# Cross-covariance attention and a mixture of adapters on one core: v in transfers of two pieces, four v buffers, paired stores, a new order

## The chip, the core and the metric

The kernel runs on one core of one Trainium2 chip. Five engines work side by side: TensorE (PE, with its weight loads shown as PEld), VectorE (DVE), ScalarE (ACT), GpSimd (POOL) and SyncE (SP). Transfers between main memory (HBM) and on-chip memory (SBUF) run on 16 DMA engines which all queues share. The metric is the device time of one execution in microseconds, as the median of several executions. The data type of inputs and output is float32.

## The reference

Four batches (B = 4), each with N = 6400 rows of C = 256 columns. The first half is attention across columns, not rows:

```
qn = q / (norm(q, axis=1) + 1e-6);  kn = k / (norm(k, axis=1) + 1e-6)
s = kn.T @ qn / tau                   # 256 x 256 per batch, sum over 6400 rows
a = softmax(s, axis=-1)
x = v @ a                             # 6400 x 256 per batch
```

The second half is a mixture of 8 low-rank adapters on the 25600 rows of x:

```
logits = x @ w_gate                   # 8 per row; the two largest are kept
w = softmax of the two
out = x + sum over the two of  w * (x @ A[e]) @ B[e]     # rank 16
```

So q, k and v are each read once (26.2 MB each) and the output is written once (26.2 MB).

## The kernel before, in words

**Tiling.** A batch's 6400 rows lie as 128 partitions x 50 chunks ("columns" in what follows: one column is 128 rows of 256 values). q and k of a batch come in three transfers each, of 17, 17 and 16 columns (`QK`, line 244; some are cut smaller by `PARTS`, line 460). v of a batch is worked on in five pieces of 10 columns; each piece comes in a transfer of its own (`V`, line 245). All these loads are issued by GpSimd at line 658 and change float32 to bfloat16 on the way, so half as many bytes are written as are read. Stores are issued by SyncE at line 1002, one for each piece of 10 columns, except that the last two pieces go out as 4, 4 and 2 columns (`FINE`, line 461).

**Steps.** For each column, `G` (lines 667 to 685) multiplies q and k into the 256 x 256 sum and, where the group of columns is not listed in `OFF` (line 463), also makes the squares of k and q on TensorE (lines 677 and 682). For groups in `OFF` the squares are made by ScalarE (`sq`, line 695) and added up by VectorE (`add`, line 701). When a batch's 50 columns are done, a chain of small steps makes the softmax (`n2`, `rsqrt`, `rq_ps`, `s`, `exp`, `aT`, `waA`, `a`). Then each v piece is transposed (`T`, line 859), copied out (`Te`), its gate logits are made (`log`, line 897), the gate steps run on VectorE and ScalarE, `Z` (line 950) makes x @ A, `Ze` scales it, `gzT` (line 973) transposes it, and five `Y` steps (lines 986 and 991) make the output of two columns each, which `Ye` copies into a y buffer. For the pieces in `MERGED` (line 470) `log` and `Z` are one step, `ZL` (line 883).

**Buffers.** Three v buffers of one piece each lie side by side in one tile (`VS`), and seven y buffers of one piece each in another (`Y`). There are six q/k buffers. A load is issued only when its buffer is free: a v buffer when the last `T` of its piece is done, a q/k buffer when the last `G` and square of its columns are done. A y buffer is free when its store has landed.

**Order.** The program is written out by a planner (`Plan`, line 69) that runs before the kernel is built: it places each step on an engine in an order that follows from its own estimates, the order of the loads (`WORDS`, line 449) and the list of buffers. On the chip each engine then works through its list strictly in that order. `HOLD` (line 456) makes a store wait until a named load has landed, although its data is ready; so reads go first and writes are kept for times in which there are few reads. `warm` steps (line 849) are matmuls without use, put where the planner expects TensorE to be idle, so that its clock is not lowered; `Clock` (line 33) decides where. GpSimd's queue has at most 8 loads under way (`OUT`).

Of the kernel before, what the change touches and what calls it, by code (L numbers as in the profile page):

```python
# [32 lines left out]
class Clock:  # L33


    WINDOW, FIRST, LOW, HIGH = 3.413, 0.31, 0.55, 0.8

    def __init__(self):
        self.busy, self.cold = [0.0], [True]

    def at(self, t):
        w = max(0, int((t - self.FIRST) / self.WINDOW) + 1)
# [6 lines left out]
    def took(self, t, us):  # L49

        end, w = t, self.at(t)
        while us > 1e-9:
            pace = 2.0 if self.cold[w] else 1.0
            step = min(us * pace, max(self.FIRST + w * self.WINDOW - end, 1e-6))
            self.busy[w] += step
            us -= step / pace
            end += step
            w = self.at(end)
        return end - t

    def idle(self, t):

        w = self.at(t)
        return t - self.FIRST - (w - 1) * self.WINDOW - self.busy[w] > self.SPARE

    SPARE = 0.8


class Plan:
# [171 lines left out]
PC = 10  # L241
NP = 5
UNITS = ((0, 4), (4, 4), (8, 2))
QK = ((0, 17), (17, 17), (34, 16))
V = (((0, 1), (1, 1), (2, 1), (3, 1), (4, 1)),) * 4
PAIRS = set()

GROUPS = ((0, 6), (6, 6), (12, 5), (17, 6), (23, 6), (29, 5), (34, 6), (40, 5), (45, 5))
ZUNITS = ((0, 3), (3, 3), (6, 2), (8, 2))
STORE = {"zl": 1, "bank": 6, "qk": 6, "v": 3, "vT": 4, "y": 7, "gate": 3, "gz": 4, "gzT": 4, "sq": 1, "ssq": 2, "port": 1}  # L250


def group_of(c):
# [187 lines left out]
def make_order(words):  # L441

    order = [("qk", 0, i) for i in range(len(QK))]
    for w in words.split():
# [1 line left out]
    return order  # L446


WORDS = ('q10 v00 v01 v02 q11 q12 v03 v04 v10 q20 v11 v12 q21 v13 q22 v14 q30 q31 v20 v21 v22 q32 v23 v24 v30 '
         'v31 v32 v33 v34')  # L450
HEAD = 5.05
COL = 1.024 * 1.17647 / 32
WARM = 150
AHEAD = 2.8

HOLD = {(0, 0): ('k', 2, 0), (0, 1): ('v', 3, 4), (0, 3): ('v', 2, 3), (1, 0): ('v', 3, 1), (1, 1): ('v', 3,
        1), (1, 3): ('v', 2, 3), (1, 4): ('v', 3, 0), (2, 2): ('v', 3, 2), (2, 3): ('v', 0, 4), (3, 0):
        ('k', 3, 2), (3, 1): ('k', 1, 1), (3, 2): ('v', 0, 1), (3, 4): ('k', 2, 1)}

PARTS = {(0, 0): ((0, 4), (4, 13)), (0, 2): ((34, 8), (42, 8)), (3, 2): ((34, 8), (42, 8))}  # L460
FINE = 2
SPLIT, SHARES = set(), ()
OFF = {(0, 0, 'k'), (0, 1, 'q'), (0, 2, 'q'), (0, 3, 'q'), (0, 5, 'q'), (0, 6, 'k'), (0, 8, 'k'), (1, 0,
        'k'), (1, 1, 'k'), (1, 2, 'k'), (1, 2, 'q'), (1, 3, 'q'), (1, 4, 'k'), (1, 5, 'q'), (1, 6, 'k'), (1,
        6, 'q'), (2, 0, 'k'), (2, 0, 'q'), (2, 3, 'q'), (2, 5, 'k'), (2, 5, 'q'), (2, 6, 'k'), (2, 7, 'q'),
        (2, 8, 'q'), (3, 0, 'k'), (3, 0, 'q'), (3, 1, 'q'), (3, 2, 'k'), (3, 2, 'q'), (3, 4, 'q'), (3, 5,
        'k'), (3, 6, 'k'), (3, 6, 'q'), (3, 7, 'k'), (3, 8, 'k')}
SQ = 0
SAFE = 0
MERGED = {(0, 1), (0, 4), (1, 0), (2, 1), (2, 2), (3, 0), (3, 2), (3, 3)}  # L470


def first_ahead(nc, names):
# [62 lines left out]
def kernel(  # L536
# [58 lines left out]
    def make_consts():  # L595
        ident = const.tile([P, P], BF16, name="ident")
        make_identity(nc, ident)
        W["ident"] = ident
        W["ident32"] = const.tile([P, P], FP32, name="ident32")
        nc.vector.tensor_copy(W["ident32"], ident)  # L600
        ones = const.tile([P, P], FP32, name="ones")
        nc.vector.memset(ones, 1.0)
        W["ones"] = ones
        neg = const.tile([P, 1], FP32, name="neg_inv_tau")
        nc.vector.memset(neg, -inv_tau)
        W["neg"] = neg
        W["zeros"] = const.tile([P, 256], BF16, name="zeros")
        nc.vector.memset(W["zeros"], 0.0)
        nc.scalar.activation(scrap[:, 0:1], neg[0:1, :], ACT.Exp)

    scrap = const.tile([1, 16], BF16, name="scrap")
# [128 lines left out]
    def do_rsqrt(s, b):  # L740
        n2 = st[b]["n2"]
        for x, w in enumerate("kq"):
            part = held.get(("bank", ("n2p", w, b)))
            if part is None:
                continue
            if all((b, g, w) in OFF for g in range(len(GROUPS))):
                nc.vector.tensor_copy(n2[:, x, :], part)
            else:
                nc.vector.tensor_tensor(out=n2[:, x, :], in0=part, in1=n2[:, x, :], op=OP.add)

        r = bat.tile([P, 2, CC], FP32, name="r0")
        nc.vector.tensor_scalar(out=r.bitcast(I32), in0=n2.bitcast(I32), scalar1=-0.5,
                                scalar2=float(0x5F1FFFF9), op0=OP.mult, op1=OP.add)
        for it, (c1, c0) in enumerate(((-0.703952253, 1.681914351), (-0.5, 1.5))):
            sq = bat.tile([P, 2, CC], FP32, name=f"sq{it}")
            nc.vector.tensor_tensor(out=sq, in0=r, in1=r, op=OP.mult)
            nc.vector.scalar_tensor_tensor(out=sq, in0=sq, scalar=c1, in1=n2,
                                           op0=OP.mult, op1=OP.mult)
            nxt = bat.tile([P, 2, CC], FP32, name=f"r{it + 1}")
            nc.vector.scalar_tensor_tensor(out=nxt, in0=sq, scalar=c0, in1=r,  # L760
                                           op0=OP.add, op1=OP.mult)
            r = nxt
        rqI = one.tile([P, CC, P], FP32, name="rqI")
        for ic in range(CC):
            nc.vector.tensor_scalar(out=rqI[:, ic, :], in0=W["ident"],
                                    scalar1=r[:, 1, ic:ic + 1], scalar2=None, op0=OP.mult)
        if inv_tau != 1.0:
            rt = bat.tile([P, CC], FP32, name="rt")
            nc.vector.tensor_scalar(out=rt, in0=r[:, 0, :], scalar1=inv_tau, scalar2=None, op0=OP.mult)
            st[b]["rk"] = rt  # L770
        else:
            st[b]["rk"] = r[:, 0, :]
        st[b]["rqI"] = rqI
# [72 lines left out]
        nc.scalar.copy(held["qk", (what, 0, 0), ""][:, 0:PARTS[0, 0][0][1], :], W[what])  # L846

    def do_warm(s, n):
        nc.tensor.matmul(bank(s, ("warm", n), [P, 512], FP32), W["ident"], W["zeros"][:, None, :].to_broadcast([P, 2, 256]),  # L849
                         start=True, stop=True)  # L850


# [16 lines left out]


    def gate_tiles(s, b, i):
        for part in ("log", "eq1", "lm", "t", "th", "mask", "g2"):
            sb(s, "gate", (b, i), [P, PC, E], FP32, part)
        for part in ("m1", "m2", "msum"):
            sb(s, "gate", (b, i), [P, PC], FP32, part)
# [30 lines left out]
    def gate_step(name):  # L906
        def f(s, b, i):
            if (b, i) in MERGED and name == "m1":
                gate_tiles(s, b, i)
            g = {part: held["gate", (b, i), part]  # L910
                 for part in ("log", "m1", "eq1", "lm", "m2", "msum", "t", "th", "mask", "g2")}
            if (b, i) in MERGED:
                g["log"] = held["zl", (b, i), ""][:, :, 0:E]
            wide = [P, PC, E]
            if name == "m1":
                nc.vector.tensor_reduce(out=g["m1"], in_=g["log"], axis=AX.X, op=OP.max)
            elif name == "eq1":
                nc.vector.tensor_tensor(out=g["eq1"], in0=g["log"], in1=g["m1"].to_broadcast(wide),
                                        op=OP.is_equal)
            elif name == "lm":  # L920
                nc.vector.scalar_tensor_tensor(out=g["lm"], in0=g["eq1"], scalar=-1e30, in1=g["log"],
                                               op0=OP.mult, op1=OP.add)
            elif name == "m2":
                nc.vector.tensor_reduce(out=g["m2"], in_=g["lm"], axis=AX.X, op=OP.max)
            elif name == "mask":
                nc.vector.tensor_tensor(out=g["mask"], in0=g["log"], in1=g["m2"].to_broadcast(wide),
                                        op=OP.is_ge)
            elif name == "msum":
                nc.vector.tensor_tensor(out=g["msum"], in0=g["m1"], in1=g["m2"], op=OP.add)
            elif name == "t":  # L930

                nc.vector.scalar_tensor_tensor(out=g["t"], in0=g["log"], scalar=2.0,
                                               in1=g["msum"].to_broadcast(wide),
                                               op0=OP.mult, op1=OP.subtract)
            elif name == "th":
                nc.scalar.activation(g["th"], g["t"], ACT.Tanh, scale=0.5)
            else:

                nc.vector.scalar_tensor_tensor(out=g["g2"], in0=g["th"], scalar=1.0, in1=g["mask"],
                                               op0=OP.add, op1=OP.mult)  # L940
# [14 lines left out]
    def do_Ze(s, b, i, u):  # L955
# [4 lines left out]
        for h in range(n // 2):  # L960
            nc.vector.tensor_tensor(  # L961
                out=pairs[:, h].rearrange("p c (e r) -> p c e r", e=E),
                in0=z[:, 2 * h:2 * h + 2, :].rearrange("p c (e r) -> p c e r", e=E),
                in1=held["gate", (b, i), "g2"][:, c + 2 * h:c + 2 * h + 2, :].to_broadcast([P, 2, E, R]), op=OP.mult)

    def do_gzT(s, b, i, u):
        c, n = UNITS[u]
# [98 lines left out]
```

## Time and profile before

| | |
|---|---|
| median of 7 executions | 253.38 us (252.92 to 253.74) |
| the profiled execution | 252.94 us, of which the span from first to last instruction is 247.3 us |
| mean granted TensorE clock | 0.978 |
| TensorE busy | 221.7 us (90%) |
| VectorE busy | 170.9 us (69%) |
| ScalarE busy | 158.1 us (64%) |
| GpSimd busy | 26.8 us (11%) |
| loads by GpSimd's queue | 48 transfers, 38.80 MB written to SBUF |
| stores by SyncE's queue | 24 transfers |
| read from HBM, written to HBM | 78.91 MB, 26.21 MB |

How to read it: the span leaves out the time before the first and after the last instruction. The DMA's busy share is the time of all packets on the 16 engines, divided by 16; as the packets of one engine overlap a little, a full DMA shows 1.00 to 1.09. The GB/s are bytes written, so that a stream of loads, which reads twice as much as it writes, shows about 214 and a stream of stores about 422. The trace also holds each DMA packet with its size, start and duration; each transfer ends with one small packet on every engine, by which one can see when the transfer has landed.

### The profile page before, as it was taken

Reading aid. Unit: us, or ns where it says so; the run is one execution under the profiler, and the core shown is the slowest. Engines: PE = TensorE matmul, PEld = TensorE weight load, DVE = VectorE, ACT = ScalarE, POOL = GpSimd, SP = SyncE. Lnnn points to the kernel's source line nnn. Section 1 sums busy time; section 2 is a strip of 40 time slices with the busy share of each in tenths; the row PEclk is TensorE's granted clock in tenths of the full one; section 3 lists DMA queues with packets and bytes.
Section 4 is the critical chain, followed back from the end, with each engine's and each line's share of the span. In section 5 each row is a group of like instructions: output and inputs, shape, how many; then the busy total and the mean of one; then the engine's idle time right before and its main releaser. Section 6 shows DMA issues by size and latency. Waiting matters only on the chain.

```text
span 247.3 us, 5994 instructions
## 1 busy us (share of the span) xinstructions
PE 221.7 (90%) x2467; PEld 196.4 (79%) x2467; DVE 170.9 (69%) x485; ACT 158.1 (64%) x294; POOL 26.8 (11%) x54
## 2 busy tenths in 40 slices
PE   0875996799999899999999899799999889999994
PEld 0463785599999788889999699679998788999993
DVE  0024376279996987885758949877997798768740
ACT  5324133275878638867775688766774776987764
POOL 7003111011000201000100302001000030000000
PEclk9979799799999999999999999999999999999999
DMA  8999999999999999999999999999999999999999
GB/s 256 214 217 210 214 222 211 214 217 220 215 209 211 319 217 211 291 290 279 213 217 259 272 217 217 209 215 213 216 213 364 425 371 225 360 318 423 429 422 413
DMA packets 10815, 65.82 MB, mean 266 GB/s; under 512 B 1219, under 2 KB 1603, under 8 KB 6180
## 3 DMA queue, kind: packets, MB, share of 16 engines
q0 software_dynamic: 6912, 38.80, 76.1%
q1 hardware_dynamic: 3540, 25.98, 25.6%
q10 hardware_dynamic: 336, 0.66, 0.8%
q8 instruction: 19, 0.31, 0.4%
q14 instruction: 8, 0.07, 0.1%
HBM read 78.91 MB, written 26.21 MB: 425 GB/s over the span
## 4 chain that ended last, share of the span: by engine, by line
DMA 57%; PE 30%; issue 9%; DVE 2%; POOL 1%; ACT 0%; POOLq 0%; DVEq 0%
DMA v<-in_v_dram 37%; DMA qk<-in_k_dram 14%; PE Y_ps L986 8%; DMA out_dram<-y 5%; PE Y_ps L991 4%; PE acc L673 4%; PE T_ps L859 3%; PE Z_ps L950 3%; PE gzT_ps L973 2%; PE ZL_ps L883 2%; PE acc L677 1%; PE acc L682 1%; POOL qk L658 1%; PE warm_ps L849 1%; DVE vT L843 1%
## 5 line engine op out<-in xcount | busy, mean ns | idle before, releaser
L673 PE MATMUL acc<-qk 128*128 128x256 bf16 x400 | 74.8, 285 | 14.8 <-DMA qk<-in_k_dram 8.6
L701 DVE TENSOR_TENSOR ssq<-ssq,sq 128x1280 f32<-128x1280 f32 (+1 forms) x27 | 43.3, 1604 | 25.1 <-ACT sq L695 24.8
L986 PE MATMUL Y_ps<-a_bf,vT 128*128 128x256 bf16 x400 | 60.0, 272 | 0.3 <-ACT y L841 0.3
L841 ACT COPY y<-Y_ps 128x512 f32<-128x512 f32 x83 | 48.0, 588 | 17.8 <-PE Y_ps L991 11.7
L695 ACT ACTIVATE sq<-qk 128x1280 f32<-128x1280 bf16 (+1 forms) x27 | 36.9, 1368 | 27.7 <-DVE ssq L701 9.9
L673 PEld LDWEIGHTS <-qk 128*128 128x128 bf16 x400 | 35.9, 103 | 19.7 <-DMA qk<-in_k_dram 10.2
L986 PEld LDWEIGHTS <-vT 128*128 128x128 bf16 x400 | 38.7, 99 | 4.7 <-issue 0.5
L991 PE MATMUL Y_ps<-ball,gzT 128*128 128x256 bf16 x200 | 38.2, 273 | 0.0
L677 PE MATMUL acc<-qk 128*128 128x128 bf16 x210 | 30.3, 227 | 0.0
L859 PE MATMUL T_ps<-ident,v 128*128 128x128 f32 x200 | 28.0, 274 | 1.4 <-DMA v<-in_v_dram 1.3
L682 PE MATMUL acc<-qk 128*128 128x128 bf16 x200 | 28.7, 227 | 0.0
L841 ACT COPY vT<-T_ps 128x512 f32<-128x512 f32 (+1 forms) x43 | 21.7, 541 | 6.8 <-PE T_ps L859 6.4
L961 DVE TENSOR_TENSOR gz<-Z_ps,gateg 128x256 bf16<-128x256 f32 x60 | 22.4, 441 | 4.3 <-PE Z_ps L950 4.2
L677 PEld LDWEIGHTS <-qk 128*128 128x128 bf16 x210 | 21.4, 102 | 3.2
L859 PEld LDWEIGHTS T_ps<-ident,v 128*128 128x128 f32 x200 | 21.9, 141 | 2.5 <-issue 0.9
L841 ACT COPY gzT<-gzT_ps 128x256 f32<-128x256 f32 (+1 forms) x45 | 14.7, 347 | 12.2 <-PE gzT_ps L973 12.1
L658 POOL DMA_DIRECT2D v<-in_v_dram x20 | 11.1, 553 | 101.7 <-PE T_ps L859 88.1
L991 PEld LDWEIGHTS <-gzT 128*128 128x128 bf16 x200 | 19.5, 98 | 2.5 <-DVE gzT L843 0.3
L973 PE MATMUL gzT_ps<-ident,gz 128*128 128x128 f32 x100 | 19.5, 281 | 1.4 <-DVE gz L961 1.0
L682 PEld LDWEIGHTS <-qk 128*128 128x128 bf16 x200 | 18.7, 102 | 2.2
L950 PE MATMUL Z_ps<-waA_sb,vT 128*128 128x128 bf16 x240 | 17.7, 219 | 0.0
L695 ACT ACTIVATE ssq<-qk 128x1536 f32<-128x1536 bf16 x8 | 11.9, 1485 | 9.0 <-DMA qk<-in_k_dram 4.5
(80 smaller groups left out, 273.8 us busy)
## 6 DMA issues: line engine op xcount, KB each, us to landing
out_dram<-y SPq DMA_DIRECT2D x18, 1280.0 KB, 12.6
v<-in_v_dram POOLq DMA_DIRECT2D x20, 640.0 KB, 25.5
qk<-in_q_dram POOLq DMA_DIRECT2D x7, 1088.0 KB, 22.3
qk<-in_k_dram POOLq DMA_DIRECT2D x7, 1088.0 KB, 26.9
qk<-in_q_dram POOLq DMA_DIRECT2D x4, 512.0 KB, 23.1
qk<-in_k_dram POOLq DMA_DIRECT2D x4, 512.0 KB, 24.7
qk<-in_q_dram POOLq DMA_DIRECT2D x2, 1024.0 KB, 31.6
qk<-in_k_dram POOLq DMA_DIRECT2D x2, 1024.0 KB, 35.6
```

The source lines that it names most:

```text
L673: nc.tensor.matmul(acc[ic][:, 0:256], kt[:, j, ic::CC], qt[:, j, :], start=c == 0, stop=False, skip_group_check=True)
L677: nc.tensor.matmul(acc[ic][:, 256:384], kt[:, j, ic::CC], kt[:, j, ic::CC], start=False, stop=False, skip_group_check=True)
L682: nc.tensor.matmul(acc[ic][:, 384:512], qt[:, j, ic * P:(ic + 1) * P], qt[:, j, ic * P:(ic + 1) * P], start=False, stop=c == NC - 1, skip_ ...
L695: nc.scalar.activation(out[:, 0:n, :], t[:, j:j + n, :], ACT.Square)
L701: nc.vector.tensor_tensor(out=t, in0=t, in1=held["sq", (w, b, g), ""][:, 0:n, :], op=OP.add)
L841: nc.scalar.copy(out, in_)
L859: nc.tensor.matmul(ps[:, j, :], vt[:, c + j, :].bitcast(FP32), W["ident32"], is_transpose=True, start=(j == 0), stop=(j == n - 1))
L950: nc.tensor.matmul(ps[:, j, :], vT_of(b, i, c + j)[:, :, ic], st[b]["aA"][:, ic, :], start=(j == 0 and ic == 0), stop=(j == n - 1 and ic = ...
L961: nc.vector.tensor_tensor(out=pairs[:, h].rearrange("p c (e r) -> p c e r", e=E), in0=z[:, 2 * h:2 * h + 2, :].rearrange("p c (e r) -> p c ...
L973: nc.tensor.matmul(ps[:, j, :], pairs[:, j * P:(j + 1) * P], W["ident32"], is_transpose=True, start=(j == 0), stop=(j == n // 2 - 1))
L986: nc.tensor.matmul(ps[:, j, :], vT_of(b, i, c + j)[:, :, ic], st[b]["a"][:, ic, :], start=(j == 0 and ic == 0), stop=False, skip_group_che ...
L991: nc.tensor.matmul(ps[:, j, :], pair[:, :, j], W["B"], start=False, stop=(j == 1), skip_group_check=True)
```

## The change

1. **v loads.** Where every v transfer was one piece, some are now two pieces (20 columns) that go into two neighbouring buffers: 14 v loads in place of 20. There are four v buffers in place of three.
2. **Stores.** Five pairs of neighbouring pieces go out in one store of 20 columns, from two neighbouring y buffers: 19 stores in place of 24.
3. **Order.** `WORDS`, `HOLD`, `OFF`, `MERGED` and `AHEAD` have new values. The loads of v come later among those of q and k, above all at the start. 30 groups of squares are on ScalarE and VectorE in place of 35; 11 pieces are `MERGED` in place of 8. The planner adds `SAFE` = 1.9 us to the time at which it expects a load, and takes squares earlier (`SQ` = 5).
4. **Memory.** Room for the fourth v buffer comes from the gate steps, which share two tiles ("ga", "gb") in place of six, from `rqI`, which shares its place with `ssqk`, and from the `zeros` tile, which is gone; warm matmuls read the identity instead.
5. **Clock.** The planner's rule for warm matmuls looks back over the last window instead of into fixed windows. 22 warm matmuls are left of 29.

```diff
-    WINDOW, FIRST, LOW, HIGH = 3.413, 0.31, 0.55, 0.8
+    WINDOW, FIRST, LOW, HIGH = 3.413, 0.31, 0.45, 0.8
...
     def idle(self, t):
-        w = self.at(t)
-        return t - self.FIRST - (w - 1) * self.WINDOW - self.busy[w] > self.SPARE
-
-    SPARE = 0.8
+        while self.worked and self.worked[0][1] < t - self.WINDOW:
+            self.worked.pop(0)
+        busy = sum(z - max(a, t - self.WINDOW) for a, z in self.worked)
+        return self.WINDOW - busy > (self.SPARE if t > self.LATE else 1.6)
+
+    SPARE, LATE = 1.3, 50.0
...
+GATE = {"eq1": "ga", "t": "ga", "th": "ga", "g2": "ga", "lm": "gb", "mask": "gb"}
-V = (((0, 1), (1, 1), (2, 1), (3, 1), (4, 1)),) * 4
-PAIRS = set()
+V = (((0, 1), (1, 2), (3, 2)), ((0, 1), (1, 1), (2, 2), (4, 1)), ((0, 1), (1, 1), (2, 1), (3, 1), (4, 1)),
+        ((0, 2), (2, 2), (4, 1)))
+PAIRS = {(0, 0), (0, 3), (1, 0), (1, 2), (2, 2)}
...
-STORE = {"zl": 1, "bank": 6, "qk": 6, "v": 3, "vT": 4, "y": 7, ...
+STORE = {"zl": 1, "bank": 6, "qk": 6, "v": 4, "vT": 4, "y": 7, ...
...
-WORDS = ('q10 v00 v01 v02 q11 q12 v03 v04 v10 q20 v11 v12 q21 v13 q22 v14 q30 q31 v20 v21 v22 q32 v23 v24 v30 '
-         'v31 v32 v33 v34')
+WORDS = ('q10 q11 v00 q12 v01 q20 v02 q21 v10 q22 v11 v12 q30 q31 v13 v20 q32 v21 v22 v23 v24 v30 v31 v32')
...
-AHEAD = 2.8
+AHEAD = 3.9
...
-HOLD = {(0, 0): ('k', 2, 0), (0, 1): ('v', 3, 4), (0, 3): ('v', 2, 3), (1, 0): ('v', 3, 1), ...
+HOLD = {(0, 0): ('k', 3, 0), (0, 1): ('k', 2, 1), (0, 2): ('v', 2, 2), (0, 3): ('v', 1, 3), (0, 4): ('v', 3,
+        0), (1, 0): ('v', 3, 3), (1, 2): ('v', 3, 2), (1, 3): ('k', 1, 2), (1, 4): ('v', 2, 2), (2, 0):
+        ('v', 0, 3), (2, 1): ('v', 1, 1), (2, 2): ('v', 2, 4), (2, 4): ('k', 2, 1), (3, 2): ('v', 0, 3)}
...
-SQ = 0
-SAFE = 0
-MERGED = {(0, 1), (0, 4), (1, 0), (2, 1), (2, 2), (3, 0), (3, 2), (3, 3)}
+SQ = 5
+SAFE = 1.9
+MERGED = {(0, 0), (0, 3), (1, 0), (1, 2), (2, 0), (2, 1), (2, 2), (2, 3), (2, 4), (3, 1), (3, 2)}
...
-        W["zeros"] = const.tile([P, 256], BF16, name="zeros")
-        nc.vector.memset(W["zeros"], 0.0)
...
-        rqI = one.tile([P, CC, P], FP32, name="rqI")
+        rqI = one.tile([P, CC, P], FP32, tag="ssqk", name="rqI")
...
-        nc.tensor.matmul(bank(s, ("warm", n), [P, 512], FP32), W["ident"], W["zeros"][:, None, :].to_broadcast([P, 2, 256]),
+        nc.tensor.matmul(bank(s, ("warm", n), [P, 512], FP32), W["ident"], W["ident"][:, None, :].to_broadcast([P, 4, P]),
...
-        for part in ("log", "eq1", "lm", "t", "th", "mask", "g2"):
+        for part in ("log", "ga", "gb"):
             sb(s, "gate", (b, i), [P, PC, E], FP32, part)
...
-            g = {part: held["gate", (b, i), part]
+            g = {part: held["gate", (b, i), GATE.get(part, part)]
```

A word of `WORDS` such as v01 names batch 0's v transfer 1, which in the new list is a transfer of two pieces (pieces 1 and 2); `HOLD` names pieces, and a piece stands for the transfer that brings it. Of a pair only the first piece's entry in `HOLD` counts.

## The prediction

> **What bounds the kernel now.** I read the page's slices and its queue table first, then a table of the stretches, then the last waits and the end.
>
> ```profile
> DMA  8999999999999999999999999999999999999999
> q0 software_dynamic: 6912, 38.80, 76.1%
> q1 hardware_dynamic: 3540, 25.98, 25.6%
> ```
>
> The 16 DMA engines are busy in every slice, and loads (76.1%) and stores (25.6%) together already exceed the span. The stretches say the same beside TensorE (columns: us, then PE, PEld, DVE, ACT, POOL busy, granted clock, DMA share, GB/s written):
>
> ```profile
> 2.00:45.00 43.00, 29.70 (x252) 22.62 (x252) 16.92 (x43) 15.04 (x14) 9.15 (x19) 0.92 1.04 226
> 45.00:74.00 29.00, 28.91 (x327) 26.05 (x328) 22.97 (x60) 19.91 (x38) 2.65 (x5) 0.94 1.04 215
> 74.00:123.00 49.00, 47.14 (x562) 42.75 (x560) 37.96 (x111) 34.83 (x70) 4.53 (x9) 1.00 1.04 254
> 123.00:183.00 60.00, 57.04 (x670) 51.52 (x668) 48.14 (x119) 43.40 (x76) 7.14 (x14) 1.00 1.04 225
> 183.00:205.00 22.00, 19.89 (x233) 17.66 (x231) 18.37 (x63) 14.09 (x33) 2.02 (x3) 1.00 1.02 362
> 205.00:223.00 18.00, 18.00 (x203) 16.64 (x201) 13.34 (x49) 14.14 (x33) 0.53 (x1) 1.00 1.04 306
> 223.00:247.00 24.00, 21.06 (x236) 19.19 (x234) 13.25 (x44) 16.48 (x36) 0.00 (x0) 0.99 1.01 422
> ```
>
> The DMA share never falls below 1.01. So nothing can be won by filling the DMA better; the time falls only if the transfers themselves cost less. It rises if the DMA runs dry, or if TensorE, nearly full from 45 us on, ends too late. How late it may end, the end of the chain and the DMA issues say:
>
> ```profile
> 243.41 0.44 PE Y_ps L986 x4
> 244.10 0.59 ACT y L841
> ...
> y<-in_q_dram SPq DMA_DIRECT2D x1, 512.0 KB, 4.0
> out_dram<-y SPq DMA_DIRECT2D x2, 256.0 KB, 7.6
> ```
>
> TensorE ends at 244.1, the last copy at 244.7, and the last store is issued then. By its packets it lands at 251.2: 6.5 us, where a lone transfer of 512 KB on SyncE's queue took 4.0, so one of 256 KB some 3.4 (0.6 less at 422 GB/s). It stands in a queue for about 3.1 us. That is TensorE's slack.
>
> **Fewer transfers.** Six v loads and five stores go. The landings (by each transfer's closing packets) give the price: with only loads moving, landings of 10 columns are 3.07 us apart, of 17 columns 5.15, of 8 columns 2.475. A line through these is 0.297 per column and 0.10 per transfer. Packets by size give more: 5120 B took 400 ns, 8704 B 663, 4096 B 324, so 24 ns a packet without its bytes; 8 packets per engine are 0.19, with the closing packet (20 ns) 0.21. But packets of one engine overlap, so I take the landings. A store's packets took 391 ns for 10240 B and 159 (median) for 4096 B, 12 ns each without bytes, about 0.10 a store with the closing one.
> Six loads: 0.6 us (0.6 to 1.3). Five stores: 0.5 us (0.15 if their packets overlap as loads' do, to 0.55). Sum: **1.1 us less DMA** (0.75 to 1.85). A 20-column packet is not in the trace; the widest is 17, and it lies on the line.
>
> The Trainium skill ("DMA: Bandwidth & Descriptors", section on the anatomy of one DMA) gives every transfer some 2.0 us beside its bytes; by that eleven transfers less would be 22 us. The trace disagrees for a queue that is never empty: 0.10.
>
> **TensorE's work.** By the two orders: 60 `log` and 60 `Z` matmuls go, 60 `ZL` come, and 56 squares of 128 columns come (22 of k, 34 of q). Prices from the trace's timeline of TensorE at full clock: `log` x20 0.50, `Z` x20 1.12, `ZL` x20 1.18, a pair of squares 0.11. So -1.5 - 3.4 + 3.5 + 3.1 = **+1.8 us**. Seven warm matmuls less count nothing: they stand where TensorE waits. VectorE loses five sums (2 x 1.49 and 3 x 1.75: -8.2 us) and nine y copies of 0.69 (-6.2) and gains zl copies (12 more on both engines, 0.41 to 0.51 each); ScalarE loses five squares (-7.0) and gains the nine y copies (+5.3). Both have 30% to spare. The two shared gate tiles and `rqI`/`ssqk` add waits only between steps that follow each other anyway: 0.
>
> **Where the new order must wait.** Up to k's first transfer of batch 1, landing at 43.3 on the fastest DMA engine and 44.7 on the slowest, loads are as before. Then come q11, k11, v00, q12, k12 and v01, the first of 20 columns: 5.15 + 5.15 + 3.07 + 4.85 + 4.85 + 6.04 = 29.1, so 72.4 and, with the slow engines' lag of some 1.6, 74.0. The first `T` of v01 starts at 74.2; what stands before it fits: 22.8 us of work from 45 us on. Before, TensorE was busy all through this stretch (28.91 of 29.00), as three v pieces came first.
> Pricing every TensorE step in the order (`G` 0.445 with both squares and 0.11 less for each pair left out, `T` 1.09, `gzT` 0.55, `Y` 0.655 for two columns) gives 202.1 us before and 204.0 after; 41.7 of the latter lies ahead of that `T`. So 162.3 remain: TensorE ends at 236.5 plus what it loses to waits. In the kernel before, the steps from 77.8 to 244.1 (166.3 us) are worth 152.9: 13.4 lost. Between loads released by `T` steps I place them: 4.9 from 80 to 144, 3.2 from 144 to 165 (waiting for q and k of batch 3 and for v20, which landed at 163.5), 1.1 to 198, 3.2 from 198 to 212 (batch 3's softmax chain), 0.4 to the end.
> After: loads have the DMA alone until v1's transfer of pieces 2 and 3 lands (121 + 1.9), the first store being held by it. Summed on from there, v14 lands at 158.9 and v21 at 175.0, where TensorE unhindered would be at 155.3 and 170.6: these force 4.4 us, about what it loses on its own by then (5), so the two don't add. Behind that I take 3 where it was 4.7, because four `Y`, a `ZL` and the `T` of the next piece now stand inside batch 3's chain (11% less work on VectorE helps). Lost: 8, so TensorE ends at **244.5**. Allowed: the DMA ends 1.1 earlier, at 250.1; less 3.4 for the store and 0.6 for the copy is 246.1. It holds, with 1.6 us to spare.
>
> **The sum.** 252.94 of the profiled execution - 1.1 = 251.8. That execution is 0.44 under the median of 253.38, so the forecast is **252.3 us** (-0.4%). Its own range is 251.5 to 252.6, by the bounds of the price (253.38 less 1.85 and less 0.75). A measurement of this kernel tells about 0.2% (0.5 us) from no change.
>
> **Clock.** The trace shows the one gap's price:
>
> ```profile
> PE acc L673 <- DMA qk<-in_k_dram: 3.3, 1, 3.3
> 45.00:48.50 3.50, 3.44 (x19) 2.78 (x20) 0.00 (x0) 1.48 (x1) 0.00 (x0) 0.51 1.06 217
> ```
>
> After 3.3 us idle the clock was 0.51 for 3.5 us: 1.7 us lost. The new waits before 74 us are 1 to 2.5 each by my sums, so I take 0; two that touch would cost the 1.7 and use up the 1.6 of slack. The Trainium skill ("TensorE: Matmul & The Clock Gate", section "Why this matters for your kernels") warns of TensorE gaps of about 3 us between bursts, which speaks against fewer warm matmuls; by it too each wait alone costs nothing.
>
> **Rivals.**
> *A, TensorE becomes the bound (slower).* If it loses as much as before, 13.2 from 74.2 on, it ends at 249.7, the copy at 250.3, the store lands at 253.7: 2.5 later than now, so 255.9. It decides from a loss of 9.6 us; slower by 0.2% needs 11.2. For it: +1.8 of work, and 29 us at the start with less to do. Against: the waits for loads between 144 and 165 and less work on VectorE and ScalarE.
> *B, the DMA runs dry near 188 us (slower).* v30 brings two pieces, so it needs two neighbouring buffers, and is issued only after `T` of 2.1 and of 2.2, at work 146.0: 74.2 + 104.3 + 5.2 = 183.7. A load that found the DMA free (issued at 198.28) moved data 3.1 us later: 186.8. What is queued (loads to v24, the stores of 0.2 and 1.4) ends at about 188.0. Beyond 1.2 us of lateness each us counts in full; likewise the four stores held by v31 need 3.5 us from its landing (182.0 to 185.5 for the one before), with 3.07 of v32 as cover: 0.4, at most 2.8. Price together 1 to 3 us: 253.3 to 255.3, typically 254.5. Before, no load had to wait for two pieces, and 25.3 us of waiting for a buffer were hidden by stores.
> *C, no gain.* The constant part is hidden by overlapping packets, or the slowest DMA engine, which landed the last store 1.6 us after the fastest, doesn't feel it; or A or B just eats it: 253.2.
>
> **How the numbers follow.** Forecast 0.48; A 0.20; B 0.15; C 0.17. So faster 0.48, same 0.17, slower 0.35. The range runs from 0.1 under the forecast's low end to A's time, with less than a tenth beyond each: 251.4 to 255.9.
>
> **What the profile after would show.** Right: 42 loads on GpSimd's queue and 19 stores; the landing of a 20-column load 6.0 us behind the one before in a stretch of loads alone; DMA share at least 1.01 in all of 2 to 247 us; the first `T` of v01 at 74 with a short wait for v's DMA; last `Y` before 246; last store 5 to 6 us from issue to landing. Wrong by A: the last store lands under 4 us after its issue. Wrong by B: a stretch near 186 to 192 or 206 to 212 with a DMA share under 0.95. A clock under 0.9 between 55 and 80 us would be the gate. What I can't see is waits of the strict order on ScalarE and VectorE, and a store that holds a y buffer longer than planned: `Y` of 3.0 needs the pair 1.0 and 1.1 landed at about 217, 2 us before it is due.

## The result

The changed kernel takes **253.98 us** (median; 253.2 to 254.27), the kernel before, measured beside it, 253.24 us. The ratio is **1.0025, with a 95% interval of 1.0018 to 1.0032**: slower by a quarter of a percent. The forecast was 252.3 us and faster. The measured time lies in the range, and on the side of rival B.

First the page of the changed kernel, its slices and its queue table (packets, MB, share of 16 engines):

```profile
DMA  8999999999999999999999999999999999999999
q0 software_dynamic: 6192, 38.80, 75.9%
q1 hardware_dynamic: 2801, 25.91, 25.1%
```

There are fewer packets (6192 for 6912, 2801 for 3540), and every slice still shows 9. A 9 stands for 90% or more, and a slice is 6 us long, so a short gap can't be seen there. The stretches of the changed kernel, cut as in the prediction and once more at 213 us (columns: us, then PE, PEld, DVE, ACT, POOL busy, clock, DMA share, GB/s written):

```profile
2.00:45.00 43.00, 28.00 (x246) 21.89 (x246) 12.70 (x29) 14.72 (x14) 8.60 (x18) 0.92 1.05 226
45.00:74.00 29.00, 24.99 (x276) 21.41 (x277) 21.10 (x46) 15.48 (x24) 1.06 (x2) 1.00 1.03 215
74.00:123.00 49.00, 48.22 (x593) 44.55 (x591) 35.07 (x112) 35.87 (x72) 5.30 (x10) 1.00 1.03 216
123.00:183.00 60.00, 57.33 (x659) 52.45 (x658) 47.10 (x130) 41.20 (x79) 6.37 (x12) 1.00 1.03 258
183.00:205.00 22.00, 20.65 (x225) 19.14 (x224) 16.57 (x64) 16.08 (x39) 1.06 (x2) 1.00 1.02 307
205.00:213.00 8.00, 8.00 (x98) 7.40 (x96) 7.77 (x30) 7.29 (x20) 1.55 (x1) 1.00 0.96 245
213.00:223.00 10.00, 10.00 (x131) 9.55 (x129) 8.15 (x29) 8.59 (x21) 0.00 (x0) 1.00 1.01 423
223.00:247.00 24.00, 22.35 (x245) 20.29 (x242) 11.43 (x42) 17.82 (x37) 0.00 (x0) 1.00 1.00 420
```

One stretch stands out: from 205 to 213 us the DMA share is 0.96, the only one under 1.00. The same stretch of the kernel before:

```profile
205.00:213.00 8.00, 8.00 (x94) 7.33 (x92) 6.94 (x25) 5.65 (x15) 0.53 (x1) 1.00 1.05 257
```

What was there to move in the changed kernel? GpSimd's timeline has its last three loads (start, us, what, idle before and releaser):

```profile
185.23 0.53 POOL L659 DMA_DIRECT2D v<-in_v_dram  x1 [19.19 <-PE T_ps L860]
191.05 0.53 POOL L659 DMA_DIRECT2D v<-in_v_dram  x1 [5.29 <-PE T_ps L860]
206.20 1.55 POOL L659 DMA_DIRECT2D v<-in_v_dram  x1 [14.63 <-PE T_ps L860]
```

These are v30, v31 and v32. By the closing packets, v31 landed between 204.8 us (fastest DMA engine) and 208.8 (slowest). The next store, the pair of pieces (1,0) and (1,1), was held until then and was issued at 209.2. The only other work, v32, was issued at 206.2, because its buffer came free with a `T` late in TensorE's list. So engines that had finished v31 had nothing to do. Two things can be counted from the packets. The 16 DMA engines stood idle for 0.5 us on average between 206 and 210 us (16 less the packets under way at each moment; before: none from 5 to 244 us). And the packets of v32, which moved alone from 210 to 212.7 us, took 0.54 us on average and up to 1.56, where the other v packets of this size took 0.40: 128 x 0.14 / 16 = 1.1 us on each engine. Together 1.6 us.

The end of the chain of work and two lines of the DMA issues:

```profile
245.13 0.23 PE Y_ps L992 x2
...
245.39 0.59 ACT y L842
```

```profile
y<-in_q_dram SPq DMA_DIRECT2D x1, 512.0 KB, 4.0
out_dram<-y SPq DMA_DIRECT2D x2, 256.0 KB, 6.9
```

TensorE ends at 245.4, the last store is issued at 246.0 and lands at 252.2, 1.0 us later than before (251.2). From issue to landing it took 6.2 us, where the prediction estimates 3.4 for a store of this size alone: it stood in a queue behind others, so the end is the DMA's.

### The profile page after: what moved, and what is told of

Its sections match the earlier page's. It is cut to its first block, busy times and chain, and to the rows that moved or that the text cites. A ratio compares the mean times of both kernels' runs of the same rounds, so it can differ in the third digit from the quotient of the medians.

```text
span 248.2 us, 5957 instructions
## 1 busy us (share of the span) xinstructions
PE 219.5 (88%) x2456; PEld 196.7 (79%) x2456; DVE 159.9 (64%) x476; ACT 157.2 (63%) x301; POOL 24.7 (10%) x49
## 3 DMA queue, kind: packets, MB, share of 16 engines
q0 software_dynamic: 6192, 38.80, 75.9%
q1 hardware_dynamic: 2801, 25.91, 25.1%
## 4 chain that ended last, share of the span: by engine, by line
DMA 49%; PE 35%; issue 8%; ACT 3%; DVE 3%; POOL 1%; ACTq 0%; POOLq 0%
DMA v<-in_v_dram 36%; PE Y_ps L987 10%; DMA qk<-in_q_dram 8%; PE Y_ps L992 5%; DMA qk<-in_k_dram 5%; PE T_ps L860 5%; PE acc L674 3%; PE gzT_ps L974 3%; PE ZL_ps L884 3%; PE Z_ps L951 2%; PE acc L678 1%; POOL qk L659 1%; ACT vT L842 1%; PE log_ps L898 1%; PE acc L683 1%
## 5 line engine op out<-in xcount | busy, mean ns | idle before, releaser
L674 PE MATMUL acc<-qk 128*128 128x256 bf16 x400 | 73.2, 279 | 17.4 <-DMA qk<-in_k_dram 10.0
L842 ACT COPY y<-Y_ps 128x512 f32<-128x512 f32 x92 | 53.2, 587 | 15.5 <-PE Y_ps L992 13.2
L702 DVE TENSOR_TENSOR ssq<-ssq,sq 128x1280 f32<-128x1280 f32 (+1 forms) x22 | 35.1, 1596 | 36.6 <-ACT ssq L696 25.6
L674 PEld LDWEIGHTS <-qk 128*128 128x128 bf16 x400 | 35.3, 101 | 20.8 <-DMA qk<-in_k_dram 11.7
L696 ACT ACTIVATE sq<-qk 128x1280 f32<-128x1280 bf16 (+1 forms) x22 | 29.9, 1359 | 16.7 <-DVE ssq L702 10.4
L678 PE MATMUL acc<-qk 128*128 128x128 bf16 x232 | 33.6, 227 | 0.0
L683 PE MATMUL acc<-qk 128*128 128x128 bf16 x234 | 33.3, 225 | 0.0
L860 PE MATMUL T_ps<-ident,v 128*128 128x128 f32 x200 | 27.0, 274 | 3.6 <-DMA v<-in_v_dram 3.5
L678 PEld LDWEIGHTS <-qk 128*128 128x128 bf16 x232 | 23.7, 102 | 3.7
L683 PEld LDWEIGHTS <-qk 128*128 128x128 bf16 x234 | 21.0, 101 | 1.1
L962 DVE TENSOR_TENSOR gz<-zl,gatega 128x256 bf16<-128x256 f32 x55 | 20.8, 445 | 0.2
L962 DVE TENSOR_TENSOR gz<-Z_ps,gatega 128x256 bf16<-128x256 f32 x45 | 17.2, 440 | 2.7 <-PE Z_ps L951 2.7
L659 POOL DMA_DIRECT2D v<-in_v_dram x15 | 9.1, 607 | 84.9 <-PE T_ps L860 66.2
```

Source lines behind the costliest of these rows:

```text
L659: loaded[s.key] = nc.gpsimd.dma_start(t[:, 0:n, :], src[b, :, c:c + n, :]).ins.name
L674: nc.tensor.matmul(acc[ic][:, 0:256], kt[:, j, ic::CC], qt[:, j, :], start=c == 0, stop=False, skip_group_check=True)
L678: nc.tensor.matmul(acc[ic][:, 256:384], kt[:, j, ic::CC], kt[:, j, ic::CC], start=False, stop=False, skip_group_check=True)
L683: nc.tensor.matmul(acc[ic][:, 384:512], qt[:, j, ic * P:(ic + 1) * P], qt[:, j, ic * P:(ic + 1) * P], start=False, stop=c == NC - 1, skip_ ...
L696: nc.scalar.activation(out[:, 0:n, :], t[:, j:j + n, :], ACT.Square)
L702: nc.vector.tensor_tensor(out=t, in0=t, in1=held["sq", (w, b, g), ""][:, 0:n, :], op=OP.add)
```

## Experiments

Theory 1: the DMA runs short of work between 205 and 213 us, because one store waits for v31, and that alone makes the loss. Theory 2: TensorE, which ends 1.3 us later than before, sets the end (rival A). Beside them stands the question whether merging transfers wins what the prediction took (0.10 us each). All experiments keep the order of every engine's list as the changed kernel has it; only what the short diffs show is changed after the order is fixed. The runs of one group share the runs of the kernel before, and groups are compared by their ratios to it; the changed kernel's is 1.0025 (the quotient of the two medians alone would be 1.0029).

**The held store let go earlier.** The pair (1,0), (1,1) waits for v30 instead of v31.

```diff
+NOW = {(1, 0): ('v', 3, 0)}
...
+    def held_now(b, i):
+        kind, d, j = NOW.get((b, i), HOLD[b, i])
+        return [k for k in loaded if k[:4] == ("load", kind, d, load_of(d, j) if kind == "v" else j)][-1]
...
-                tc.add_manual_dep(r.ins, loaded[held_by(plan, b, i)],
+                tc.add_manual_dep(r.ins, loaded[held_now(b, i)],
```

> Only the wait of one store changes: the pair of pieces (1,0) and (1,1) is held by the landing of v30 (at 199.6 us in the profile after) instead of v31 (208.8). All orders stay. Theory 1 (the DMA ran short of work between 205 and 213 us, which cost 0.5 us of idle engines and 1.1 us of packets of v32 that took up to 1.5 us instead of 0.4): the DMA share of 205 to 213 rises to at least 1.00, v32's packets are back at about 0.40 us, and the time falls by 1.0 to 1.6 us against the changed kernel, to 252.4 to 253.0, ratio to before 0.997 to 0.999. Theory 2 (TensorE, ending at 245.35, sets the end): no change, 253.7 to 254.2. A loss instead (over 254.3) would say that the store now takes the DMA from v31, and T of (3,2) waits for it.

Measured: **252.48 us, ratio 0.9972 (0.996 to 0.9983)**. One wait turned a loss of 0.25% into a gain of 0.28%. The stretches of this kernel:

```profile
205.00:213.00 8.00, 8.00 (x103) 7.45 (x101) 7.51 (x29) 7.12 (x18) 1.56 (x1) 1.00 1.01 388
213.00:223.00 10.00, 10.00 (x128) 9.49 (x125) 8.35 (x32) 8.70 (x23) 0.00 (x0) 1.00 1.02 379
```

The DMA share is 1.01, 388 GB/s are written where it was 245, the idle time of the DMA engines is gone (0.03 us from 5 to 244), and v32's packets take 0.40 us on average. The last store lands at 250.6 for 252.2: 1.6 us, as counted. Theory 1 holds here in place and in size.

**The same store held longer**, by v32.

```diff
-NOW = {(1, 0): ('v', 3, 0)}
+NOW = {(1, 0): ('v', 3, 4)}
```

> The same store is held longer: by the landing of v32 (215.7 us in the profile after) instead of v31 (208.8). SyncE's queue is strict, so the stores behind it wait too. Theory 1: the stretch in which the DMA has nothing to store grows from about 209 to 212 to about 209 to 218, less the earlier landing of v32 with the DMA to itself (some 213): 2 to 5 us more than the changed kernel, 256 to 259, and the stretch shows a DMA share far under 1. Theory 2: the stores at the end have 2.8 us to spare (6.2 us from issue to landing, where 3.4 would do), so the first 2.8 us of lateness cost nothing; 254 to 256.

Measured: 254.79 us, ratio 1.0058 (1.0043 to 1.0073), so 0.8 us over the changed kernel by the ratios. The size is under what theory 1 gave and inside what theory 2 gave. The stretches:

```profile
205.00:213.00 8.00, 8.00 (x99) 7.40 (x98) 7.57 (x28) 7.27 (x19) 1.55 (x1) 1.00 0.87 238
213.00:223.00 10.00, 10.00 (x129) 9.53 (x127) 8.35 (x30) 8.35 (x21) 0.00 (x0) 1.00 0.85 355
```

The DMA shares of 0.87 and 0.85 are theory 1's sign: the engines were idle for 2.8 us, 2.3 more than in the changed kernel. Why the loss is smaller than expected can be read from the packets. v32 landed at 213.7, and the store left at 214.0, 4.9 us later than in the changed kernel. But on the idle engines its first packet started 0.8 us after the issue (at 214.85), where in the changed kernel, with v32 still moving, that took 3.6 us (209.15 to 212.72). So its data came only 2.1 us later; I had expected the gap to last until about 218. And v32's packets were delayed less (0.45 us on average, 0.4 us in all for 1.1). In the profiled execution 2.3 - 0.7 = 1.6 is what came out (last landing 253.7 for 252.2); that execution, 255.55, was the slowest of the four. The last store took 7.5 us from issue to landing, so TensorE did not set the end there. The time of this run alone doesn't decide between the theories; the next run does.

**Less work for TensorE at the end.** The adapter product of pieces 1 to 4 of batch 3 is left out.

```diff
-                    start=(j == 0 and ic == 0), stop=False, skip_group_check=True)
-        for j in range(2):
+                    start=(j == 0 and ic == 0), stop=(b, i) > (3, 0) and j == ic == 1, skip_group_check=True)
+        for j in range(0 if (b, i) > (3, 0) else 2):
```

> The adapter product (the last two matmuls of each Y step, line 992) is left out for pieces 1 to 4 of batch 3, so the output of these rows lacks the adapters' part. That takes 20 x 0.22 = 4.4 us from TensorE, all of it after 219 us, behind the stretch of theory 1. Theory 1 and a full DMA from 213 us on: no change within 0.3 us (253.7 to 254.3), though TensorE ends some 2 to 4 us earlier. Theory 2: the time falls by up to the 2.8 us by which the store then no longer has to wait for TensorE; at least 1.5 us, to 252.5 or less.

Measured: 253.77 us, ratio 1.002 (1.0009 to 1.0031), not to be told from the changed kernel's 1.0025. The last stretch of this kernel:

```profile
223.00:247.00 24.00, 18.00 (x203) 16.21 (x201) 11.26 (x41) 16.45 (x37) 0.00 (x0) 0.93 1.00 422
```

TensorE works 18.0 us there instead of 22.35, and its last `Y` is done at 241.0 us. The last store is issued at 242.7 instead of 246.0, but lands no earlier (252.3 for 252.2): from issue to landing it now takes 9.6 us. Theory 2 falls.

**Stores split.** The five stores of 20 columns go out as two of 10 each.

```diff
-        for rows in SHARES if (b, i) in SPLIT else (P,):
-            r = nc.sync.dma_start(out_v[b, p:p + rows, lo:lo + n, :], Y[p:p + rows, at_y:at_y + n, :])
+        for x in range(0, n, PC):
+            m = min(PC, n - x)
+            r = nc.sync.dma_start(out_v[b, :, lo + x:lo + x + m, :], Y[:, at_y + x:at_y + x + m, :])
...
-            p += rows
+            p += 1
```

> The five stores of 20 columns go out as two stores of 10 columns each, one right behind the other, in the same place of the same order. By the price in the prediction (0.10 us a transfer) the time rises by 0.5 us against the changed kernel, to 254.5; if packets overlap as those of loads do, by 0.15 us. The rival C of the prediction (the constant part of a transfer is hidden) says 0.0. A fall would say that wide store packets hurt.

Measured: 254.48 us, ratio 1.0042 (1.003 to 1.0055): 0.4 us over the changed kernel by the ratios, 0.09 a store. The intervals of the two just overlap, so this alone would not decide; with the next group it does.

**The first experiment again, and the split on top of it.** To see the merging without the gap, the next three ran together on the first experiment's kernel: unchanged; with the v loads of 20 columns as two of 10; and with loads and stores split.

> The kernel of the first experiment once more, as the base for the two beside it on the same chip: ratio to before 0.996 to 0.999, as in its first runs (0.9972), if its gain is not one of a chip or of chance.

```diff
-        loaded[s.key] = nc.gpsimd.dma_start(t[:, 0:n, :], src[b, :, c:c + n, :]).ins.name
+        for x in range(0, n, PC if what == "v" else n):
+            m = min(PC, n - x) if what == "v" else n
+            loaded[s.key] = nc.gpsimd.dma_start(t[:, x:x + m, :], src[b, :, c + x:c + x + m, :]).ins.name
```

> On top of the first experiment's kernel, each v transfer of 20 columns goes out as two transfers of 10 columns, one right behind the other, into the same buffers: 48 loads in place of 43, all else in the same order. By the price in the prediction (0.10 us a transfer, from landings; up to 0.21 from packets) the time rises by 0.5 us (up to 1.1) against the first experiment's kernel, to 253.0. If the constant part of a load is hidden by overlapping packets: 0.0 to 0.2. A fall would say that it is worth more to have the first half of a pair early (its T can start 3 us sooner) than to save a transfer.

> On top of that, the five stores of 20 columns are also two of 10 each. What is left of the change is then the new order, the fourth buffer and the new waits, with as many transfers as before (48 loads, 24 stores) and the store of (1,0) no longer held by v31. If the merging is all that the change can win, as predicted (the order can fill nothing that was empty), this equals the kernel before within 0.2%: 253.1 to 253.6, and 0.9 to 1.1 us over the first experiment's kernel. If it is still faster than before by 0.2% or more, the order wins something by itself.

| kernel | us | ratio to before |
|---|---|---|
| store let go earlier, again | 252.48 | 0.9967 (0.9955 to 0.998) |
| and loads split | 253.00 | 0.9989 (0.998 to 0.9998) |
| and loads and stores split | 253.37 | 1.0004 (0.9995 to 1.0012) |
| kernel before | 253.29 | 1 |

Five loads are worth 0.52 us and five stores 0.37: 0.10 and 0.07 each. The intervals of neighbouring rows touch, so each price by itself is rough; the two steps together (0.9967 against 1.0004) are clear. With as many transfers as before, the new order, the fourth buffer and all other parts of the change give the time of the kernel before. So in this kernel the merging is all that the change can win, and the held store took it away and more. (The Trainium skill, "DMA: Bandwidth & Descriptors", section on the anatomy of one DMA, has some 2 us as the fixed time of one transfer by GpSimd, for setup and completion. In a queue that is never empty, these runs show a twentieth of that, 0.10, as what one load more adds to the time.)

**Three transfers fewer still.** On the first experiment's kernel the last two parts of q and of k of batch 3 are one transfer each, and two stores of piece (3,3) are one.

```diff
+        if (b, i) == (3, 2) and what != "v":
+            if c > QK[i][0]:
+                loaded[s.key] = loaded[("load", what, b, i) + PARTS[b, i][0]]
+                return
+            n = QK[i][1]
...
+        if (i, c) == (3, 0) and n == 4:
+            return
+        if (i, c) == (3, 4):
+            c, n = 0, 8
```

> On top of the first experiment's kernel, three more transfers are merged: the last q and the last k part of batch 3 come as one transfer of 16 columns each instead of two of 8, and the first two stores of piece (3,3) go out as one of 8 columns. At 0.10 us a transfer this is 0.3 us less, 252.2 to 252.3, ratio to before about 0.996. Against it: the first 8 columns of q and k are complete some 5 us later (173.3 instead of 168.0 us), just when TensorE comes to them (about 173), and the store of piece (3,3) leaves 1.3 us later with 4 us of stores queued ahead of it; if TensorE then runs late enough for v30 to come late, the time rises by up to 1 us.

Measured: **252.32 us, ratio 0.9954 (0.9937 to 0.997)**, the lowest of all, though its interval overlaps that of the kernel it stands on. Its end shows a gap of another kind:

```profile
223.00:247.00 24.00, 22.64 (x247) 20.53 (x245) 11.70 (x44) 17.80 (x37) 0.00 (x0) 1.00 0.97 406
```

The DMA share is 0.97, and the engines are idle for 0.6 us between 236 and 244, most of it from 241.0 to 242.7: here the DMA does have to wait for output to store. Just then the merged store of (3,3) comes. It was issued at 241.8; in the first experiment's kernel its first four columns left at 237.1. TensorE also ended 1.2 us later in this run (245.6 for 244.5). So the merged store itself makes at least part of the gap, by holding data back until its second half is done; how much is TensorE's, as in rival A, no run separates.

## Why the prediction was wrong

**The bound: right.** The DMA sets the end before and after; emptying TensorE's list at the end did nothing.

**The price of a transfer: right in size, wrong in count.** 0.10 us for a load and 0.10 for a store; measured 0.10 and 0.07 to 0.09. A 20-column packet took 776 ns, on the line through the others. But v comes in 15 transfers, not 14 (3, 4, 5 and 3), and the queue has 43 loads, so five loads go and not six; the description of the change above has the same miscount. The term should have been 1.0 us instead of 1.1; splitting measured 0.9.

**TensorE: nearly right.** Forecast end 244.5, measured 245.4; loss to waits 8 forecast, 8.9 measured (245.4 less 236.5), of which 0.9 is the first `T` of v01, which came at 75.1 instead of 74.2. It waited as foreseen (v01 landed at 72.8 to 74.6, forecast 72.4 to 74.0), and the waits of `T` for v's loads sum to 3.5 us, 1.3 the longest. The granted clock was 1.00 from 45 to 74 us: no gap cost anything there. The 1.6 us of slack were enough. (The losses that the prediction places in the kernel before add up to 12.8 us and not to 13.4, and rival A takes 13.2; the forecast doesn't rest on this.)

That the clock stayed up was partly luck. Just before 45 us TensorE waited 3.5 us for k in the changed kernel, longer than the 3.3 us after which the kernel before ran at 0.51, and lost nothing. In the first experiment's profile the same wait, also 3.5 us, came with half the clock from 44.4 to 51.2 us (0.89 in the mean of this stretch; columns as above):

```profile
45.00:74.00 29.00, 27.47 (x277) 23.49 (x278) 21.14 (x47) 15.15 (x24) 1.05 (x2) 0.89 1.02 214
```

The length of the wait alone doesn't decide it here. That kernel was the faster one all the same, as TensorE wasn't the bound.

**The step that failed: the sum, which gave nothing for a DMA that runs dry.** It takes 1.1 us from the time before and so lets the DMA stay full to its end; that TensorE would be in time held. I had seen the place: rival B says that the stores held by v31 "need 3.5 us from its landing, with 3.07 of v32 as cover: 0.4, at most 2.8". The error is that v32 was taken as queued behind v31. It was not: v32 needs a buffer that `T` of (3,0) frees, and that came at 206.2 us, when the fast DMA engines had finished v31 and the last store before it. By my own list this `T` ends at 165.6 us of work, which is 198.1 us in time without any loss (74.2 + 165.6 - 41.7), and with all 8 us of loss that I gave TensorE it comes at 206. The prediction never placed it; it only counted its 3.07 us. So the cover was empty when it was needed, and B's price was 1.6 us and not 0.4. B had a chance of 0.15, with 254.5 as its typical time; 254.0 came. B's sign, a share under 0.95 near 206 to 212 us, shows only in a narrow window (columns as above):

```profile
207.00:211.00 4.00, 4.00 (x54) 3.62 (x52) 3.77 (x17) 3.53 (x11) 0.76 (x1) 1.00 0.94 241
```

B's two waits before data moves were misread, too. The 3.5 us after a store's release were taken on busy DMA engines; on idle ones it was 0.8 (second experiment). And the load that "found the DMA free" and moved data 3.1 us later did so among stores, in a stretch with a DMA share of 1.02.

**The other half of B did not come true.** Near 188 us, where v30 was to come late, the DMA share stayed at 1.02: v30 was issued at 185.2, 1.5 us later than my sum, and the stores of (0,2), (1,4) and (2,0) filled the time.

**What was not settled.** Of the 1.6 us, 0.5 are idle engines and 1.1 are long packets. That both go when the store is let go earlier is shown; why the packets of v32 took up to 1.56 us is open: see below.

## What to carry to other kernels

Where the DMA is full, its time is the sum of its packets plus every moment in which some engine has nothing queued, so for each wait that holds transfers back, list what else is already issued at that moment, not what stands next in the order. Transfers held back as a reserve should wait for something that lands clearly before the queue runs out; moving one such wait by one load was worth 1.3 to 1.5 us here by the ratios, more than all the merging. A saving of 0.1 us a transfer is real, but small enough that a single hole in the queue turns its sign.

## What I had not expected of the hardware

GpSimd took 1.55 us to issue v32, where each of the other v loads of the changed kernel's end took 0.53. It took as long in the first experiment's kernel (1.56), in the same place:

```profile
205.34 1.56 POOL L662 DMA_DIRECT2D v<-in_v_dram  x1 [14.62 <-PE T_ps L863]
```

But there the packets of v32 took 0.40 us, with stores moving beside them, and in the changed kernel, with next to nothing beside them, up to 1.56. The other runs agree: the packets are long in the three that keep the gap (0.45 to 0.56 us on average in the second, third and fourth experiment) and not in the four that build on the first. So the long packets go with the gap, and not with the load, its size or the long issue. VectorE was busy for 7.5 to 7.8 of the 8 us from 205 to 213 us in both the changed kernel and the first experiment's. What lengthens them stays open. A wait for the issue to be written out would be one explanation, but by the profile the issue ended at 207.75, before the first of these packets started (208.46), and no run tested it.
